# Second MLP put into the list scheduler, with a shorter product in its clock; the values of the square go to SBUF

## The chip, the cores and the metric

The kernel runs on one core of a Trainium2 chip. The metric is device time in microseconds (us), lower is better; a kernel is timed in several runs and the median counts. One further execution is recorded by the hardware profiler; its rows are the ones read here. Engines are named as the profile names them: PE is TensorE's matmul, PEld its weight load, DVE is VectorE, ACT is ScalarE, POOL is GpSimd, SP the engine that issues the DMAs.

## The reference, cut to what matters

Attention through 32 packed positions per head, then two MLPs over 4608 tokens. The change is in the second MLP, `_moe2_ref`: a product, SoLU (the input times its softmax), a layer norm, a product.

```python
def _moe_ref(x, w_in, w_out):                 # first MLP, d_ff 2048, ELU
    h = x @ w_in
    g = np.where(h > 0.0, h, np.exp(np.minimum(h, 0.0)) - 1.0)
    return g @ w_out

def _moe2_ref(x, w_in, w_out, g_ln):          # second MLP, d_ff 1024
    h = x @ w_in
    h_max = np.max(h, axis=-1, keepdims=True)
    e = np.exp(h - h_max)
    sm = e / (np.sum(e, axis=-1, keepdims=True) + 1e-09)
    solu = h * sm
    mu = np.mean(solu, axis=-1, keepdims=True)
    var = np.mean((solu - mu) ** 2, axis=-1, keepdims=True)
    ln = (solu - mu) / np.sqrt(var + 1e-06) * g_ln
    return ln @ w_out
```

## The kernel before

**Tiles.** Every fp32 product is made of three fp32r products: each operand is split into a rounded part (hi) and the rest (lo), and hi*hi, lo*hi and hi*lo are added up in PSUM. The first MLP works on half a batch of 288 tokens at a time (b, half) and on 16 blocks f of 128 hidden columns; its name for a step is b_half_f, so `fe7_1_10` is the ELU buffer of batch 7, half 1, block 10. A step is the product `h` (6 matmuls), ELU on ACT and DVE (`fe`), a split into `ghi` and `glo`, and 12 matmuls into `acc`. The result goes to DRAM in `x2_dram` and is read back as `x2raw` in tiles of 512 tokens.

**The second MLP** works on 36 tiles i of 128 tokens (NTT = 36), four to an `x2raw` tile. For each of them:

- `split_x2` (L504): hi on ACT, lo on DVE (`x2hi`, `x2lo`).
- `h2_mm` (L509): 24 matmuls of 512 columns into a PSUM tile of two banks. There are three such tiles: `misc` has one buffer and `acc` two, and the tiles take them in turn, so product i+3 takes the tile of product i (product 1 takes that of product 0).
- `solu_ln` (L520): negated row maximum (`nm`, DVE), exponential with row sum (`e`, ACT), reciprocal (`sm`, `r`, DVE), `z` = h times softmax with row sum (DVE), the square with its sum (ACT, L535), the variance (`sq`, DVE), its power -1/2 (POOL), `ln` (DVE). Of the square only its sum is used; its values were written over the product in PSUM.
- `t2_blocks` (L543): a transposition of 32x32 blocks (`lnB`, DVE) and 16 copies that put the blocks in place (`lnX`), half on DVE (L555) and half on ACT (L557).
- `t2_a` (L560): the split of the transposed tile, `lnT`: hi on ACT, lo on DVE. There are two buffers, so tile i+2 waits until product i is done.
- `out_mm` (L566): 24 matmuls `o`, the first 16 of which read only hi; a copy `y` to SBUF (ACT) and the store (SP). The last tile does its 512 columns in two halves.

**What sets the order.** The attention and the first MLP are nodes of a list scheduler (`order`, L924): each node has an engine, a duration in the planner's own clock, needs, buffers that it takes and lets go, and perhaps a due time; the scheduler lays each engine's nodes in one order that is then emitted as it stands, for PE, DVE, ACT and SP. Before the change the scheduler's last nodes were the load of the first `x2raw` tile, the splits of tiles 0 and 1, and `h2_mm(0)`. Everything behind that was called by hand at the end of the kernel (L1023 to L1048): there PE follows the written order (`h2_mm(i + 3)`, then `out_mm(i)`), while DVE, ACT, POOL and SP are ordered by the framework's own scheduler, which may also put their instructions among those of the first MLP.

Of the kernel before, what the change touches and what calls it, by code (L numbers as in the profile page):

```python
# [34 lines left out]
def attention_mlp_kernel(ctx: ExitStack, tc: tile.TileContext, q, k, v, v_tail, p,  # L35
# [484 lines left out]
    def solu_ln(i):  # L520
        o = last.pop(("h2", i)).rearrange("p a c -> p (a c)")
        nm = small.tile([P, 1], F32, tag="nm", name=f"nm2_{i}")
        dve.tensor_reduce(out=nm, in_=o, axis=AX.X, op=ALU.max, negate=True)  # L523
        e = work.tile([P, 5 * 4 * D], F32, tag="k", name=f"e3_{i}", bufs=1)[:, 0:DFF2]
        sm = small.tile([P, 1], F32, tag="sm", name=f"sm2_{i}")
        act.activation(e, o, AF.Exp, bias=nm, accum_out=sm)
        dve.tensor_scalar(out=sm, in0=sm, scalar1=1e-9, scalar2=None, op0=ALU.add)
        r = small.tile([P, 1], F32, tag="r", name=f"r2_{i}")
        dve.reciprocal(r, sm)
        z = work.tile([P, 5 * 4 * D], F32, tag="q", name=f"z{i}", bufs=1)[:, 0:DFF2]  # L530
        su = small.tile([P, 1], F32, tag="su", name=f"su{i}")
        dve.scalar_tensor_tensor(out=z, in0=o, scalar=r, in1=e, op0=ALU.mult, op1=ALU.mult, accum_out=su)  # L532
        dve.tensor_scalar(out=su, in0=su, scalar1=-1.0 / DFF2, scalar2=None, op0=ALU.mult)
        sq = small.tile([P, 1], F32, tag="sq", name=f"sq{i}")
        act.activation(o, z, AF.Square, bias=su, accum_out=sq)  # L535
        dve.tensor_scalar(out=sq, in0=sq, scalar1=1.0 / DFF2, scalar2=1e-6, op0=ALU.mult, op1=ALU.add)
        rs = small.tile([P, 1], F32, tag="rs", name=f"rs{i}")
        nc.gpsimd.tensor_tensor(out=rs, in0=sq, in1=mhalf, op=ALU.pow)
        ln = work.tile([P, DFF2], F32, tag="stage", name=f"ln{i}", bufs=2)
        dve.tensor_scalar(out=ln, in0=z, scalar1=su, scalar2=rs, op0=ALU.add, op1=ALU.mult)  # L540
        last["ln", i] = ln

    def t2_blocks(i):  # L543
# [5 lines left out]
        tv = t.rearrange("p (c a n) -> p c a n", a=4, n=NP)
        ov = o.rearrange("p (c n) -> p c n", n=P)  # L550
        for r in range(4):
            for a in range(4):
                x, y = ov[a * NP:(a + 1) * NP, :, r * NP:(r + 1) * NP], tv[r * NP:(r + 1) * NP, :, a]
                if (r + a) % 4 < 2:
                    dve.tensor_copy(x, y)  # L555
                else:
                    act.copy(x, y)  # L557
        last["t2", i] = o

    def t2_a(i):  # L560
        o = last.pop(("t2", i))
        t = slot(f"lnT{i}", [P, 2, 8, P], f"wo{6 + i % 2}", F32R)
        both(split(t[:, 0].rearrange("p c n -> p (c n)"), t[:, 1].rearrange("p c n -> p (c n)"), o))
        last["lnT", i] = t

    def out_mm(i):  # L566
        t = last.pop(("lnT", i))
        n = DM if i < NTT - 1 else DM // 2
        for c in range(0, DM, n):
            o = h_ps(f"o{i}_{c}")[:, 0:n]  # L570
            for x in range(2):
                for kk in range(8):
                    w, cs = wo2[kk // 2], slice((kk % 2) * DM + c, (kk % 2) * DM + c + n)
                    pe.matmul(o, t[:, x, kk], w[:, 0, cs], start=x + kk == 0, stop=x == 1 and kk == 7)  # L574
                    if x == 0:
                        pe.matmul(o, t[:, 0, kk], w[:, 1, cs], start=False, stop=False)  # L576
            y = work.tile([P, DM], F32, tag="at", name=f"y{i}_{c}", bufs=3)[:, 0:n]
            act.copy(y, o)
            sp.dma_start(out=out[i * P:(i + 1) * P, c:c + n], in_=y)
# [309 lines left out]
    def order():  # L889
# [194 lines left out]
```

## Time and profile before

| | before |
|---|---|
| median of 3 runs | 1145.37 us (1145.16 to 1147.82) |
| profiled execution, its own time | 1142.79 us |
| its span, first to last instruction | 1141.0 us |
| PE busy | 1114.4 us (98%) |
| DVE busy | 868.5 us (76%) |
| ACT busy | 750.7 us (66%) |
| POOL busy | 20.4 us (2%) |
| mean granted TensorE clock | 0.994 |

The profiled execution is 1.8 us longer than its span, and 2.6 us under the median of the runs. PE's busy share counts overlapping matmuls whose ends are modelled; where PE loses time is read from the starts of its matmuls. The second MLP's first product starts at 731.54 us and its last matmul at 1137.55 us.

### The profile page before, as it was taken

What the parts mean: (1) busy time and instruction counts of PE and PEld (TensorE: products, weight loads), DVE (VectorE), ACT (ScalarE), POOL (GpSimd) and SP (SyncE); (2) the same over time, 40 slices, a digit from 0 to 9 for tenths busy, and PEclk for the clock granted to TensorE, in tenths of its full rate; (3) what the DMA queues carried; (4) which work ended last, traced back from release to release, by engine and by line L of the source; (5) the groups of instructions that cost most, each with busy time, mean ns of one, the idle gap of its engine ahead of it and who ended that gap; (6) DMA issues with size and microseconds to landing.
All of it is one profiled execution on the core that took longest, in us unless ns stands there. A gap on an engine that the chain in (4) does not pass through costs nothing.

```text
span 1141.0 us, 21041 instructions
## 1 busy us (share of the span) xinstructions
PE 1114.4 (98%) x8164; PEld 984.1 (86%) x8164; DVE 868.5 (76%) x1956; ACT 750.7 (66%) x1627; POOL 20.4 (2%) x42
## 2 busy tenths in 40 slices
PE   8799999999999999999999999999999999999997
PEld 7588898899899899899899899878888888888886
DVE  5899897678777778777778644588877878878775
ACT  4688865666666765666665555567776776676674
POOL 0000000000000000000000000000000000000000
PEclk9899999999999999999999999999999999999999
DMA  9957334024133124233122322610202101000001
GB/s 344 342 174 260 105 104 125 24 82 139 59 121 121 59 103 139 77 103 121 59 101 99 111 95 65 215 52 34 65 19 65 56 28 65 19 28 20 28 28 38
DMA packets 56116, 111.07 MB, mean 97 GB/s; under 512 B 4432, under 2 KB 32336, under 8 KB 54224
## 3 DMA queue, kind: packets, MB, share of 16 engines
q1 hardware_dynamic: 56016, 109.73, 28.3%
q8 instruction: 64, 1.05, 0.4%
q14 instruction: 36, 0.29, 0.1%
HBM read 77.14 MB, written 32.57 MB: 96 GB/s over the span
## 4 chain that ended last, share of the span: by engine, by line
PE 54%; DVE 22%; ACT 15%; issue 6%; POOL 1%; DMA 1%; POOLq 0%; SPq 0%; ACTq 0%; DVEq 0%
PE acc L64 11%; PE acc L66 10%; PE acc L65 10%; ACT lnX L557 6%; PE h L64 6%; PE h L66 6%; PE h L65 6%; DVE lnB L547 4%; PE m L348 3%; DVE ln L540 2%; DVE z L532 2%; ACT h L535 2%; DVE lnT L154 2%; DVE nm L523 2%; PE s L348 2%
## 5 line engine op out<-in xcount | busy, mean ns | idle before, releaser
L64 PE MATMUL acc<-ghi,wo 128*128 128x288 f32 x1024 | 305.9, 299 | 0.6 <-DVE part L484 0.3
L66 PE MATMUL acc<-glo,wo 128*128 128x288 f32 x1024 | 301.6, 295 | 1.2 <-DVE glo L449 1.2
L65 PE MATMUL acc<-ghi,wo 128*128 128x288 f32 x1024 | 301.5, 294 | 0.0
L64 PEld LDWEIGHTS acc<-ghi,wo 128*128 128x128 f32 x1024 | 192.2, 188 | 22.0 <-ACT fe L433 9.1
L66 PEld LDWEIGHTS acc<-glo,wo 128*128 128x128 f32 x1024 | 192.4, 188 | 1.7 <-DVE glo L449 1.7
L65 PEld LDWEIGHTS acc<-ghi,wo 128*128 128x128 f32 x1024 | 192.3, 188 | 0.0
L574 PE MATMUL o<-wo,lnT 128*128 128x512 f32 (+1 forms) x592 | 185.0, 385 | 4.5 <-ACT lnT L152 4.5
L446 ACT CAST ghi<-fe 128x288 fp32r<-128x288 f32 x256 | 110.2, 431 | 103.5 <-DVE fe L439 102.7
L439 DVE SCALAR_TENSOR_TENSOR fe<-fe,h 128x288 f32<-128x288 f32 x256 | 115.3, 451 | 77.1 <-ACT fe L434 73.8
L557 ACT COPY lnX<-lnB 32x256 f32<-32x256 f32 x288 | 116.3, 404 | 78.1 <-DVE lnB L547 65.5
L64 PE MATMUL h<-AT,M 128*128 128x288 f32 x512 | 155.7, 304 | 10.6 <-DVE fe L439 9.0
L433 ACT ACTIVATE fe<-h 128x288 f32<-128x288 f32 x256 | 104.7, 409 | 91.3 <-PE h L66 85.9
L65 PE MATMUL h<-AT,M 128*128 128x288 f32 x512 | 151.6, 296 | 0.0
L66 PE MATMUL h<-AT,M 128*128 128x288 f32 x512 | 151.2, 295 | 0.3 <-DVE AT L154 0.3
L449 DVE TENSOR_TENSOR glo<-fe,ghi 128x288 fp32r<-128x288 f32 x256 | 115.3, 451 | 44.1 <-ACT ghi L446 41.8
L574 PEld LDWEIGHTS o<-wo,lnT 128*128 128x128 f32 x592 | 110.7, 189 | 27.4 <-ACT lnT L152 5.3
L64 PEld LDWEIGHTS h<-AT,M 128*128 128x128 f32 x512 | 96.3, 188 | 33.0 <-DVE fe L439 14.5
L434 ACT ACTIVATE fe<-fe 128x288 f32<-128x288 f32 x256 | 113.9, 445 | 8.0
L576 PE MATMUL o<-wo,lnT 128*128 128x512 f32 (+1 forms) x296 | 113.8, 386 | 0.0
L64 PE MATMUL h<-wi,x2hi 128*128 128x512 f32 x288 | 112.3, 390 | 1.3 <-ACT h L535 1.3
L66 PE MATMUL h<-wi,x2hi 128*128 128x512 f32 x288 | 112.1, 389 | 0.0
L65 PE MATMUL h<-wi,x2lo 128*128 128x512 f32 x288 | 112.1, 389 | 0.0
(101 smaller groups left out, 1613.5 us busy)
## 6 DMA issues: line engine op xcount, KB each, us to landing
k<-in_k SPq DMA_DIRECT2D x32, 288.0 KB, 3.5
q<-in_q SPq DMA_DIRECT2D x16, 576.0 KB, 4.5
x_dram<-x SPq DMA_DIRECT2D x32, 288.0 KB, 2.8
x2raw<-x_dram SPq DMA_DIRECT2D x9, 1024.0 KB, 5.6
out_x<-y SPq DMA_DIRECT2D x35, 256.0 KB, 2.0
raw_wi<-in_w_in SPq DMA_DIRECT2D x8, 1024.0 KB, 9.6
v<-in_v SPq DMA_DIRECT2D x16, 512.0 KB, 5.2
w_dram<-w SPq DMA_DIRECT2D x16, 512.0 KB, 2.9
```

What stands on the lines that cost most here:

```text
L64: pe.matmul(o, a[0], b[0], start=start, stop=False)
L65: pe.matmul(o, a[1], b[0], start=False, stop=False)
L66: pe.matmul(o, a[0], b[1], start=False, stop=stop)
L348: pe.matmul(o[u * NP:(u + 1) * NP, r], w[rows, u, :], x[rows, u, :], start=True, stop=True)
L433: act.activation(e, o[:, 0:HS], AF.Relu, scale=-1.0)
L434: act.activation(e, e, AF.Exp, scale=-1.0)
L439: dve.scalar_tensor_tensor(out=e, in0=e, scalar=-1.0, in1=o[:, 0:HS], op0=ALU.add, op1=ALU.max)
L446: act.copy(ghi, e)
L449: dve.tensor_tensor(out=glo, in0=e, in1=ghi.bitcast(F32), op=ALU.subtract)
L557: act.copy(x, y)
L574: pe.matmul(o, t[:, x, kk], w[:, 0, cs], start=x + kk == 0, stop=x == 1 and kk == 7)
L576: pe.matmul(o, t[:, 0, kk], w[:, 1, cs], start=False, stop=False)
```

## The change

All of the second MLP becomes nodes of the list scheduler, for all 36 tiles. `solu_ln`, `t2_blocks` and `t2_a` are cut into one function per step, POOL becomes an engine of the planner, and a product counts 4.6 us in the planner's clock (H2_US; the one node of it that was there counted 5.6). The square (L546 after) writes its values into the SBUF tile `ln`, which `so_ln` overwrites later, so the PSUM tile of the product is let go by `z` and not by the square. In the last tile 12 of the 16 block copies are DVE's, 4 ACT's. The calls by hand at the end are gone. The number of matmuls, of bytes and of the other steps stays.

```diff
+    def so_z(i):
+        z = last["z", i] = work.tile([P, 5 * 4 * D], F32, tag="q", name=f"z{i}", bufs=1)[:, 0:DFF2]
...
+    def so_sqr(i):
+        sq = last["sq", i] = small.tile([P, 1], F32, tag="sq", name=f"sq{i}")
+        ln = last["ln", i] = work.tile([P, DFF2], F32, tag="stage", name=f"ln{i}", bufs=2)
+        act.activation(ln, last["z", i], AF.Square, bias=last["su", i], accum_out=sq)
-        act.activation(o, z, AF.Square, bias=su, accum_out=sq)
...
+    ENGINES = PE, DVE, ACT, SP, POOL = "PE", "DVE", "ACT", "SP", "POOL"
+    LATENCY = {PE: 0.2, DVE: -0.02, ACT: -0.03, SP: 1.9, POOL: 0.1}
...
-    node(("h2", 0), PE, 5.6, [("spD", "x2", 0)] + [("wi2", j) for j in range(4)],
-         lambda: h2_mm(0), takes=[("misc", "h2")], due=end_due + 2)
+    end_due = FIRST_US + STEP_US * len(steps) + 2
+    H2_US = 4.6
...
+    for i in range(NTT):
+        out_due = end_due + (4 + 2 * i) * H2_US
+        h2_due = end_due + i * H2_US if i < 4 else out_due - 7 * H2_US
+        bank = ("misc" if i % 3 == 0 or i == 1 else "acc", ("h2", i))
...
+        node(("h2", i), PE, H2_US, [("spD", "x2", i)] + ([("wi2", j) for j in range(4)] if i == 0 else []),
+             lambda i=i: h2_mm(i), takes=[bank], due=h2_due,
...
+        node(("so_max", i), DVE, 1.22, [("h2", i)], lambda i=i: so_max(i))
+        node(("so_exp", i), ACT, 1.33, [("so_max", i)], lambda i=i: so_exp(i), takes=[e3])
+        node(("so_z", i), DVE, 1.5, [("so_rec", i)], lambda i=i: so_z(i), takes=[z], lets=[e3, bank])
+        node(("so_sqr", i), ACT, 1.33, [("so_z", i)], lambda i=i: so_sqr(i), takes=[ln])
...
+                eng = DVE if (r + a) % 4 < 2 or i == NTT - 1 and (r + a) % 4 < 3 else ACT
+                moves.append(node(("t2m", i, r, a), eng, 0.29 if eng == DVE else 0.4,
...
+            node(("out", i, c), PE, H2_US * n / DM, [("spD", "lnT", i)] + ([("wo2", j) for j in range(4)] if i == 0 else []),
+                 lambda i=i, c=c, n=n: out_mm(i, c, n), takes=[o], lets=[lnt], due=out_due + (c > 0) * 2.7)
...
-    ctx.enter_context(tc.manual_schedule(engines={mybir.EngineType.PE}))
-    solu_ln(0)
-    both(split_x2(2))
-    h2_mm(1)
...
-        out_mm(i)
```

What the scheduler makes of it is seen in the order of instructions. On PE the order is the same up to the end of the first MLP; there `h` of step 7_1_15 now stands ahead of the second MLP's first product and no longer behind it; products 5 to 8 each stand one place earlier among the `o` products (h2_3, o_0, h2_4, h2_5, o_1, h2_6, o_2, h2_7, o_3, h2_8, o_4, o_5, h2_9, o_6), and from there on the order is that of before. On SP `x2raw1`, the second tile of 512 tokens, was issued ahead of the two halves of `wo2_3`, the last weights of the second product, and now stands behind them.

The first place is ACT's queue in the last steps of the first MLP (`x2hi0` and `x2hi1` are hi of the first and second 512 tokens, `e3_0` the exponential of the second MLP's tile 0). Before:

```order
L433 ACTIVATE fe7_1_10_9541<-h7_1_10_9521 128x288
L152 CAST x2hi0_9472<-x2raw0_9470 128x4x128 x2
L434 ACTIVATE fe7_1_10_9541<-fe7_1_10_9541 128x288
L152 CAST x2hi0_9472<-x2raw0_9470 128x4x128
L446 CAST ghi7_1_10_9546<-fe7_1_10_9541 128x288
L152 CAST x2hi0_9472<-x2raw0_9470 128x4x128
L433 ACTIVATE fe7_1_11_9574<-h7_1_11_9549 128x288
L152 CAST x2hi1_9840<-x2raw1_9838 128x4x128 x4
L434 ACTIVATE fe7_1_11_9574<-fe7_1_11_9574 128x288
```

After, to the same step's ELU and then at the end of the first MLP:

```order
L433 ACTIVATE fe7_1_10_9541<-h7_1_10_9521 128x288
L434 ACTIVATE fe7_1_10_9541<-fe7_1_10_9541 128x288
L152 CAST x2hi0_9472<-x2raw0_9470 128x4x128
L446 CAST ghi7_1_10_9546<-fe7_1_10_9541 128x288
L152 CAST x2hi0_9472<-x2raw0_9470 128x4x128
...
L433 ACTIVATE fe7_1_15_9704<-h7_1_15_9671 128x288
L434 ACTIVATE fe7_1_15_9704<-fe7_1_15_9704 128x288
L446 CAST ghi7_1_15_9708<-fe7_1_15_9704 128x288
L152 CAST x2hi1_9649<-x2raw1_9647 128x4x128 x4
L528 ACTIVATE e3_0_9734,sm2_0_9735<-h2_0_9679,nm2_0_9732 128x1024
```

The splits of `x2raw0` moved behind both halves of the ELU of step 7_1_10 and stand one at a time between the steps; the four of `x2raw1` moved from the middle of step 7_1_11 to behind the last step.

The second place is the end of DVE's queue, the second MLP's tiles 34 and 35 (`lnB` is the transposition, `nm2` the maximum, `lnX` the block copies, `lnT` the lo part that the product needs). Before:

```order
L547 STREAM_TRANSPOSE lnB34_13033<-ln34_12973 128x1024
L523 TENSOR_REDUCE nm2_35_13052<-h2_35_13005 128x1
L555 COPY lnX34_13035<-lnB34_13033 32x8x32 x8
L527 TENSOR_SCALAR sm2_35_13055<-sm2_35_13055 128x1
L529 RECIPROCAL r2_35_13058<-sm2_35_13055 128x1
L532 SCALAR_TENSOR_TENSOR z35_13060,su35_13061<-h2_35_13005,r2_35_13058,e3_35_13054 128x1024
L533 TENSOR_SCALAR su35_13061<-su35_13061 128x1
L154 TENSOR_TENSOR lnT34_13099<-lnX34_13035,lnT34_13099 128x1024
```

After:

```order
L565 STREAM_TRANSPOSE lnB34_13029<-ln34_13013 128x1024
L523 TENSOR_REDUCE nm2_35_13056<-h2_35_12985 128x1
L576 COPY lnX34_13058<-lnB34_13029 32x8x32 x2
L154 TENSOR_TENSOR lnT33_13026<-lnX33_12964,lnT33_13026 128x1024
L533 TENSOR_SCALAR sm2_35_13061<-sm2_35_13061 128x1
L534 RECIPROCAL r2_35_13067<-sm2_35_13061 128x1
L576 COPY lnX34_13058<-lnB34_13029 32x8x32
L539 SCALAR_TENSOR_TENSOR z35_13072,su35_13073<-h2_35_12985,r2_35_13067,e3_35_13060 128x1024
L541 TENSOR_SCALAR su35_13073<-su35_13073 128x1
L576 COPY lnX34_13058<-lnB34_13029 32x8x32 x5
```

The copies of tile 34 are spread around the steps of tile 35, and the lo part of tile 33 stands where DVE had waited for the exponential. The same pattern fills nearly all tiles from 10 on. The third place is ACT's queue beside it, the same two tiles. Before:

```order
L557 COPY lnX34_13035<-lnB34_13033 32x8x32 x8
L526 ACTIVATE e3_35_13054,sm2_35_13055<-h2_35_13005,nm2_35_13052 128x1024
L578 COPY y32_0_13096<-o32_0_13071 128x512
L152 CAST lnT34_13099<-lnX34_13035 128x1024
L535 ACTIVATE h2_35_13005,sq35_13064<-z35_13060,su35_13061 128x1024
```

After:

```order
L528 ACTIVATE e3_35_13060,sm2_35_13061<-h2_35_12985,nm2_35_13056 128x1024
L574 COPY lnX34_13058<-lnB34_13029 32x8x32 x7
L546 ACTIVATE ln35_13107,sq35_13106<-z35_13072,su35_13073 128x1024
L594 COPY y32_0_13113<-o32_0_13031 128x512
L574 COPY lnX34_13058<-lnB34_13029 32x8x32
L152 CAST lnT34_13120<-lnX34_13058 128x1024
```

The exponential of tile 35 moved from behind the eight copies of tile 34 to ahead of them.

## Rows read from the trace of the kernel before

**Rows 1.** Stretches: PE, PEld, DVE, ACT, POOL busy (x instructions), clock, DMA, GB/s.
```profile
780.00:1108.00 328.00, 328.00 (x1448) 271.69 (x1448) 265.81 (x565) 226.40 (x446) 16.45 (x30) 1.00 0.11 37
1119.00:1132.00 13.00, 8.53 (x30) 6.23 (x29) 8.48 (x22) 9.69 (x20) 0.55 (x1) 0.87 0.12 42
```
**Rows 2.** Timeline of PE, first MLP's end: start, us, instruction [idle before <-releaser].
```profile
717.45 0.30 PE L64 MATMUL h<-AT,M 128*128 128x288 f32 x1
...
719.83 0.29 PE L64 MATMUL h<-AT,M 128*128 128x288 f32 x1
...
722.46 0.40 PE L64 MATMUL h<-AT,M 128*128 128x288 f32 x1
...
726.65 0.40 PE L64 MATMUL h<-AT,M 128*128 128x288 f32 x1 [1.55 <-DVE fe L439]
```
**Rows 3.** Timeline of PE, from the first MLP's last matmul to o_0.
```profile
742.46 0.29 PE L66 MATMUL acc<-glo,wo 128*128 128x288 f32 x1
743.52 0.50 PE L64 MATMUL h<-wi,x2hi 128*128 128x512 f32 x1 [0.77 <-ACT h L535]
...
755.22 0.50 PE L64 MATMUL h<-wi,x2hi 128*128 128x512 f32 x1 [0.51 <-ACT h L535]
...
760.79 0.39 PE L574 MATMUL o<-wo,lnT 128*128 128x512 f32 x1
```
**Rows 4.** Timeline of PE: h2_35, o_32, o_34 and o_35 start.
```profile
1103.51 0.39 PE L64 MATMUL h<-wi,x2hi 128*128 128x512 f32 x1
...
1108.95 0.39 PE L574 MATMUL o<-wo,lnT 128*128 128x512 f32 x1
...
1122.59 0.50 PE L574 MATMUL o<-wo,lnT 128*128 128x512 f32 x1 [2.60 <-ACT lnT L152]
...
1131.83 0.39 PE L574 MATMUL o<-wo,lnT 128*128 128x256 f32 x1 [1.88 <-ACT lnT L152]
```
**Rows 5.** Timeline of ACT, splits of `x2raw0` and `x2raw1`.
```profile
720.09 1.14 ACT L152 CAST x2hi<-x2raw 128x512 fp32r<-128x512 f32 x2 [1.24 <-DMA x2raw<-x_dram]
...
723.60 2.17 ACT L152 CAST x2hi<-x2raw 128x512 fp32r<-128x512 f32 x4
```
**Rows 6.** Timeline of DVE, end of the queue: tile 34's and tile 35's maximum.
```profile
1105.64 1.19 DVE L523 TENSOR_REDUCE nm<-h 128x1 f32<-128x1024 f32 x1
...
1114.44 0.81 DVE L540 TENSOR_SCALAR ln<-z,su,rs 128x1024 f32<-128x1024 f32 x1 [0.73 <-POOL rs L538]
...
1116.46 1.19 DVE L523 TENSOR_REDUCE nm<-h 128x1 f32<-128x1024 f32 x1
```
**Rows 7.** Timeline of ACT, tile 35: copies of tile 34, exponential, hi of tile 35.
```profile
1116.57 3.31 ACT L557 COPY lnX<-lnB 32x256 f32<-32x256 f32 x8 [3.04 <-DVE lnB L547]
1119.91 1.11 ACT L526 ACTIVATE e<-h,nm 128x1024 f32<-128x1024 f32 x1
...
1130.73 1.04 ACT L152 CAST lnT<-lnX 128x1024 fp32r<-128x1024 f32 x1
```
**Rows 8.** Timeline of DVE, tile 0's maximum and `z`.
```profile
737.22 1.23 DVE L523 TENSOR_REDUCE nm<-h 128x1 f32<-128x1024 f32 x1 [2.29 <-PE h L66]
...
740.72 1.28 DVE L532 SCALAR_TENSOR_TENSOR z<-h,r,e 128x1024 f32<-128x1024 f32 x1
```
**Rows 9.** Timeline of SP's queue: `x2raw0` and `x2raw1`, `wo2_3`.
```profile
712.19 5.98 SPq L499 DMA_DIRECT2D x2raw<-x_dram  x2
720.82 0.88 SPq L197 DMA_DIRECT2D wo<-w_dram  x2
```
**Rows 10.** Groups from 700 us on: busy us, mean ns | idle before, releasers.
```profile
L555 DVE COPY lnX<-lnB 32x256 f32<-32x256 f32 x288 | 81.5, 283 | 3.6
...
L547 DVE STREAM_TRANSPOSE lnB<-ln 128x1024 f32<-128x1024 f32 x36 | 44.8, 1245 | 1.1
L154 DVE TENSOR_TENSOR lnT<-lnX,lnT 128x1024 fp32r<-128x1024 f32 x36 | 44.1, 1224 | 10.7 <-ACT lnT L152 10.7
...
L535 ACT ACTIVATE h<-z,su 128x1024 f32<-128x1024 f32 x36 | 40.2, 1117 | 30.3 <-DVE su L533 30.3
```

More of the change, by code (lines that the diff above doesn't have):

```diff
@@ L527, in solu_ln, with so_rec @@
+    def so_rec(i):
+        sm = last.pop(("sm", i))
+        r = last["r", i] = small.tile([P, 1], F32, tag="r", name=f"r2_{i}")
         dve.tensor_scalar(out=sm, in0=sm, scalar1=1e-9, scalar2=None, op0=ALU.add)
-        r = small.tile([P, 1], F32, tag="r", name=f"r2_{i}")
         dve.reciprocal(r, sm)
-        z = work.tile([P, 5 * 4 * D], F32, tag="q", name=f"z{i}", bufs=1)[:, 0:DFF2]
-        su = small.tile([P, 1], F32, tag="su", name=f"su{i}")
-        dve.scalar_tensor_tensor(out=z, in0=o, scalar=r, in1=e, op0=ALU.mult, op1=ALU.mult, accum_out=su)
@@ L549, in t2_blocks @@
[L549 to L579, printed above, removed]
@@ L585, in attention_mlp_kernel, with t2_move @@
-    ENGINES = PE, DVE, ACT, SP = "PE", "DVE", "ACT", "SP"
+    def t2_move(i, r, a, eng):
+        if ("lnX", i) not in last:
+            last["lnX", i] = big.tile([P, 4 * HS], F32, tag="AT", name=f"lnX{i}", bufs=3)[:, 0:DFF2]
+        tv = last["lnB", i].rearrange("p (c a n) -> p c a n", a=4, n=NP)
+        ov = last["lnX", i].rearrange("p (c n) -> p c n", n=P)
+        x, y = ov[a * NP:(a + 1) * NP, :, r * NP:(r + 1) * NP], tv[r * NP:(r + 1) * NP, :, a]
+        if eng is act:
+            act.copy(x, y)
+        else:
+            dve.tensor_copy(x, y)
@@ new lines, in t2_split, with out_mm @@
+    def t2_split(i):
+        t = last["lnT", i] = slot(f"lnT{i}", [P, 2, 8, P], f"wo{6 + i % 2}", F32R)
+        return split(t[:, 0].rearrange("p c n -> p (c n)"), t[:, 1].rearrange("p c n -> p (c n)"), last.pop(("lnX", i)))
+    def out_mm(i, c, n):
+        t = last["lnT", i]
+        o = last["y", i, c] = h_ps(f"o{i}_{c}")[:, 0:n]
+        for x in range(2):
+            for kk in range(8):
+                w, cs = wo2[kk // 2], slice((kk % 2) * DM + c, (kk % 2) * DM + c + n)
+                pe.matmul(o, t[:, x, kk], w[:, 0, cs], start=x + kk == 0, stop=x == 1 and kk == 7)
+                if x == 0:
+                    pe.matmul(o, t[:, 0, kk], w[:, 1, cs], start=False, stop=False)
@@ L586, in attention_mlp_kernel, with y_copy, y_store @@
+    def y_copy(i, c, n):
+        y = work.tile([P, DM], F32, tag="at", name=f"y{i}_{c}", bufs=3)[:, 0:n]
+        act.copy(y, last.pop(("y", i, c)))
+        last["y", i, c] = y
+    def y_store(i, c, n):
+        sp.dma_start(out=out[i * P:(i + 1) * P, c:c + n], in_=last.pop(("y", i, c)))
+    ENGINES = PE, DVE, ACT, SP, POOL = "PE", "DVE", "ACT", "SP", "POOL"
     CAPS = dict(misc=1, acc=2, h=2, fe=2, ghi=4, glo=4, at=3, AT=3, cv=2, stage=2, xo=2)
-    LATENCY = {PE: 0.2, DVE: -0.02, ACT: -0.03, SP: 1.9}
+    LATENCY = {PE: 0.2, DVE: -0.02, ACT: -0.03, SP: 1.9, POOL: 0.1}
```

94 lines of the change are left out of this document (51 added, 43 removed).

## The prediction

> **What bounds the kernel now.** I read the busy time of each engine by stretches first, then the starts of PE's matmuls where a stretch is not full, then, around each hole, the queue of the engine that PE waited for. In the stretch from 780 to 1108 us PE is busy in 328.00 of 328.00 us, at a granted clock of 1.00 [rows 1]. A product of 24 matmuls takes 5.44 us there, from the start of h2_35 at 1103.51 to that of o_32 at 1108.95 [rows 4], so a tile, with its two products, takes PE 10.88 us. The matmuls stay what they are, so nothing can be gained in this stretch. What can be gained are holes, and they lie in three places.
>
> First, the last steps of the first MLP. The product h of two steps starts 2.38 us apart when nothing waits (717.45 to 719.83); the next two follow at 722.46 and 726.65, that is 2.63 and 4.19 us later [rows 2]. Lost: 0.25 + 1.81 = 2.06 us. The wait is for DVE's `fe`, and the reason stands in ACT's queue: at 720.09 two `x2hi` casts that waited 1.24 us for the load of `x2raw0`, and at 723.60 four more of 2.17 us for the second tile of tokens [rows 5], each between the two halves of one step's ELU, as the order shows.
>
> Second, the first products of the second MLP. h2_1 starts at 743.52, 1.06 us after the last matmul before it instead of the 0.13 us at which such matmuls follow each other (18 of them in a step's 2.38); from h2_1 to h2_3 it is 11.70 us instead of 2 x 5.44 = 10.88; from h2_3 to o_0 5.57 instead of 5.44 [rows 3]. Lost: 0.93 + 0.82 + 0.13 = 1.88 us. Both waits are for ACT L535, the square, which still wrote over the product in the one `misc` tile.
>
> Third, the end. o_32 starts at 1108.95; o_35, three products later, would start at 1108.95 + 16.32 = 1125.27 and starts at 1131.83 [rows 4]. Lost: 6.56 us. o_34 and o_35 both wait for hi of `lnT`, 2.60 and 1.88 us. In the stretch 1119 to 1132 the granted clock is 0.87 [rows 1]: with levels of 2.4 and 1.2 GHz that is 26% of 13 us at the lower one, 3.4 us, of which half, 1.7 us, is loss. PE had stood still for 2.60 us before the clock fell, so this is part of the same hole. The cause is a lag. h2_35 is done at 1108.95, yet its maximum starts at 1116.46 [rows 6], 7.5 us later, with no wait in front of it: DVE came to it late. DVE's round, from tile 34's maximum to tile 35's, takes 1116.46 - 1105.64 = 10.82 us [rows 6], just under PE's 10.88, so a lag once there is never worked off. While PE has products of other tiles it costs nothing; after the last h2 it is the path.
>
> **The change, part by part.**
>
> *Splits of x2.* The `x2raw0` casts move behind the first ELU half; the wait for the load now hides in slack, since the ELU of 7_1_10 is done before it and `glo` of that step is wanted only at the end of the product h of 7_1_12, about 723.0. The cast that starts at 720.09 delays `ghi` by 0.6 us to about 721.1. The four casts for the second tile go behind step 7_1_15. What is late next: `x2raw1` is now behind `wo2_3` in SP's queue. That load starts at 720.82 and takes SP 0.88 us [rows 9], so `x2raw1` is issued at about 721.7 and no longer at 717.6 (the end of the merged row, 718.17, less one issue). The nearest row for its flight is `x2raw0`, also issued right behind 1 MB of weights: 712.19 to 720.09, 7.9 us, hence 729.6. By my walk PE then runs from 719.83 without a hole: four h-and-acc pairs of 2.38 (the steps 11 to 14 of half 1) and h of 7_1_15 (0.8) bring h2_0 to about 730.2, and ACT reaches the four casts at about 732.2, two microseconds of ELU later. Margin 2.6 us. I take the loss of 2.06 as gone; the ends are nothing gained, and all of it.
>
> *Bank of h2.* h2_0 runs 730.2 to 735.6; twelve matmuls each for three steps end at 740.4. In the trace h2_0 ended at 731.54 + 5.44 = 736.98, the maximum started 0.24 us later, and `z` ended 4.78 us after that start (740.72 + 1.28 - 737.22) [rows 8], with an ELU step in between on both engines that is now gone. So `z` lets the bank go at 740.6 at worst, some 0.5 us sooner without that ELU, and PE wants it at 740.4; the square, on the path before, is off it. For h2_3 the same 5.0 us after h2_1's end at 745.8 make 750.8, and it is wanted at 751.3. I take 1.88 as gone. The ends: zero, and 1.88. Sum of both at the start: 3.94, o_0 at about 756.9 and not 760.79.
>
> The square's own time: on the row SBUF to PSUM takes 1117 ns [rows 10]; the cast of the same 128x1024, SBUF to SBUF, takes 1040 [rows 7]. I cost the new destination at nothing; at 0.1 us it would be hidden under ACT's slack (226.40 of 328 us busy [rows 1]) in all but the last tile. The Trainium skill (ScalarE: Activation LUTs, Step-by-step: what each stage is for) says that ScalarE writes faster to PSUM than to SBUF, a rule against this edit; by it the square would grow, and the sum would lose that once, at the end. The two rows do not show such a difference.
>
> *Order in the steady stretch.* DVE is busy 265.81 us in 328, 8.8 us a tile [rows 1]. Its round of 10.82 holds 2.0 us of waits: some 1.2 for the exponential, which stood behind eight copies on ACT, 0.73 for POOL and the rest for the square. In the new order the lo part of an older tile, 1224 ns [rows 10], fills the first wait, and the exponential stands ahead of the copies. My round: 8.8 + 0.73 + 0.2 = 9.7 us. Bounds: 8.8 with no wait, 10.82 with all. Either is under 10.88, and DVE now starts without a lag, since the maxima of tiles 1 to 3 wait for PE. So each maximum starts when its product ends, and PE never waits: hi of tile i is ready before h2_(i+2) ends, a product and more ahead of o_i.
>
> *End.* Let E be the end of h2_35, and count from E. DVE: maximum 0.2 to 1.3 (the next instruction starts 1.11 behind it), two copies at 0.29 to 1.9, lo of 33 to 3.1, two small steps and a copy to 3.8, `z` to 5.2, row sum 5.3, five copies 6.8. ACT: exponential 1.5 to 2.7, seven copies at 0.41 to 5.6, square to 6.8, `y32` 7.4, one copy 7.8, hi of 34 to 8.9. o_34 wants that at 10.88: no wait. DVE goes on: variance 7.2, POOL, `ln` 7.9 to 8.75, transposition 1245 ns [rows 10] to 10.0, three copies 10.9, lo of 34 12.2 (its product wants lo after 16 matmuls, at 14.5), nine copies 14.9; ACT hi of 35, 1.04 [rows 7], to 16.0. o_35 wants it at 16.32: no wait, by 0.3 us. The 12 copies on DVE cost 3.5 us and not 2.35, but ACT's four end at 13.4 and were the longer side. So all 6.56 us go, the lower clock too, as PE no longer stands still. Ends: zero if a lag of 7 us stays, 6.56 if none does.
>
> *Sum.* 2.06 + 1.88 + 6.56 = 10.5 us. Against the profiled execution, 1142.79 - 10.5 = 1132.3. The runs' median lies 2.6 us above that execution, so I carry the difference over to it: 1145.37 - 10.5 = **1134.9 us**, 0.9% less.
>
> **Rivals.** *A, the start gives nothing.* `x2raw1` lands late, and DVE and ACT stand in queue: both have its four splits ahead of tile 0's maximum and exponential, so every microsecond of landing after 732.2 is PE's. For it: the load moved 4 us back, behind 1 MB. Against it: the 2.6 us of margin. At 4 us of delay the 3.94 are gone: 1145.4 - 6.6 = 1138.8.
>
> *B, the end gives nothing.* A lag of DVE arises again in tiles 4 to 8, where the new order has the maximum of tile 6 ahead of that of tile 5 and mixes in the splits of the third token tile, and stays. Against it: a round of 9.7 works off 1.2 us a tile. 1145.4 - 3.9 = 1141.4.
>
> *C, slower.* The new round of DVE and ACT is longer than PE's 10.88, since each engine stands in its one queue for steps of three tiles at once. Then each of 34 tiles adds the excess to the lag, and the end pays it all: at 11.5 us it is 34 x 0.62 = 21 us in place of the 6.6 of now, 1145.4 - 3.9 - 6.6 + 21 = 1156. It loses from a round of 10.88 + 10.5/34 = 11.2 on. Against it: the sum of the steps is 1.5 us short of that.
>
> *D, no change.* In tiles 4 to 8 PE meets products whose `lnT` is not ready, o_4 and o_5, which now follow each other with no h2 between: my walk has hi of tile 5 some 5 us ahead of its product, and the planner's 4.6 us against the true 5.44 makes it think DVE scarcer than it is, not less so. If both wait a whole product, 10.9 us, the gain is eaten: 1145.8.
>
> **How the numbers follow.** Forecast 0.70, with a range of its own of 1132 to 1138; A 0.12, B 0.07, C 0.05, D 0.06. The range 1131.5 to 1140.5 holds forecast and A, and leaves out B, C and D, 0.18. About 0.3%, 3.4 us, is what a measurement here can tell from no change: faster means under 1141.9. Forecast, A and most of B (0.05) are faster: 0.87. The rest of B and D are the same: 0.08. C is slower: 0.05.
>
> **What would show it.** In the new profile h of 7_1_11 to 7_1_15 start 2.38 us apart; no PE wait names the square; o_0 starts at 757 or so; the maximum of a late tile starts within 0.5 us of its product's end, with a wait for PE in front of it; o_34 and o_35 have no wait in front, and the clock is 1.00 to the end. It would be wrong if the four casts of `x2raw1` wait for a DMA, if DVE's round is over 10.88, or if a PE wait for `lnT` shows up among o_1 to o_6.

## The result and the profile after

The changed kernel takes 1134.13 us (median of 5 runs, 1132.46 to 1135.35), the kernel before, run beside it, 1145.37 us (5 runs, 1144.6 to 1147.82): ratio 0.9898, 95% interval 0.9882 to 0.9914, 11.2 us less. The forecast was 1134.9.

The profiled execution of after is 1135.35 us long with a span of 1133.6 us, only 7.4 us less than before's 1141.0. The rest of the difference lies ahead of everything that the change touches. The product h of step 7_1_10, which in both kernels follows the same PE instructions, starts at 717.45 us in before's trace [rows 2] and at 720.67 in after's. From there to the end of the span before takes 423.55 us and after 412.93: 10.62 us less, where 10.5 were forecast. The 3.2 us are taken up under the last heading. Below, stretches of two traces are compared from a common instruction, not by the clock of the span.

The two stretches of [rows 1] in after's trace, and between them a third, from 1111 to 1124 us, up to the last tile:

```profile
780.00:1108.00 328.00, 328.00 (x1449) 271.70 (x1448) 276.35 (x577) 233.23 (x452) 20.74 (x31) 1.00 0.13 45
1111.00:1124.00 13.00, 13.00 (x59) 10.78 (x58) 10.59 (x28) 8.99 (x18) 0.55 (x1) 1.00 0.11 40
1119.00:1132.00 13.00, 11.41 (x73) 10.24 (x72) 5.05 (x12) 4.58 (x9) 0.00 (x0) 1.00 0.17 59
```

PE is full to 1124 and beyond, at a clock of 1.00; the last line includes the end, where there is nothing left to do. The steps of the first MLP, which answer to [rows 2], are evenly spaced at 2.38 to 2.40 us:

```profile
720.67 0.30 PE L64 MATMUL h<-AT,M 128*128 128x288 f32 x1
...
723.05 0.30 PE L64 MATMUL h<-AT,M 128*128 128x288 f32 x1
...
725.45 0.30 PE L64 MATMUL h<-AT,M 128*128 128x288 f32 x1
...
727.83 0.30 PE L64 MATMUL h<-AT,M 128*128 128x288 f32 x1
```

h2_1 and o_0, which answer to [rows 3], and o_32 and its predecessor h2_35, to [rows 4]. None has a wait in front of it:

```profile
743.55 0.30 PE L66 MATMUL acc<-glo,wo 128*128 128x288 f32 x1
743.68 0.39 PE L64 MATMUL h<-wi,x2hi 128*128 128x512 f32 x1
...
760.02 0.39 PE L588 MATMUL o<-wo,lnT 128*128 128x512 f32 x1
...
1102.74 0.39 PE L64 MATMUL h<-wi,x2hi 128*128 128x512 f32 x1
...
1108.18 0.39 PE L588 MATMUL o<-wo,lnT 128*128 128x512 f32 x1
```

ACT's splits of `x2raw0` and `x2raw1` (compare [rows 5]): the first still waits for its load, but behind the ELU; the four of the second follow the last step and wait for nothing.

```profile
722.11 0.45 ACT L434 ACTIVATE fe<-fe 128x288 f32<-128x288 f32 x1
723.22 0.62 ACT L152 CAST x2hi<-x2raw 128x512 fp32r<-128x512 f32 x1 [0.66 <-DMA x2raw<-x_dram]
...
735.36 2.18 ACT L152 CAST x2hi<-x2raw 128x512 fp32r<-128x512 f32 x4
```

DVE at the end (compare [rows 6]). The maximum of tile 35 now stands waiting for PE; before it started 7.5 us late with no wait:

```profile
1097.50 1.22 DVE L523 TENSOR_REDUCE nm<-h 128x1 f32<-128x1024 f32 x1 [1.21 <-PE h L66]
...
1108.38 1.23 DVE L523 TENSOR_REDUCE nm<-h 128x1 f32<-128x1024 f32 x1 [1.22 <-PE h L66]
...
1120.32 2.68 DVE L576 COPY lnX<-lnB 32x256 f32<-32x256 f32 x9
```

And ACT's hi of tile 35 (compare [rows 7]), which o_35 waits for:

```profile
1123.08 1.05 ACT L152 CAST lnT<-lnX 128x1024 fp32r<-128x1024 f32 x1 [1.56 <-DVE lnX L576]
```

It ends at 1124.13 and o_35 starts at 1108.18 + 16.32 = 1124.50, on time, with 0.37 us to spare.

What DVE waited for between 900 and 1100 us shows where the lag comes from (waits by line; total us, times, longest). Before:

```profile
DVE sm L527 <- ACT e L526: 13.5, 11, 1.2
DVE ln L540 <- POOL rs L538: 10.5, 14, 1.1
DVE sq L536 <- ACT h L535: 7.7, 14, 1.4
...
```

After:

```profile
DVE nm L523 <- PE h L66: 15.3, 16, 2.4
DVE ln L558 <- POOL rs L554: 9.8, 17, 0.7
DVE sq L550 <- ACT ln L546: 0.8, 1, 0.8
```

Before, DVE waited 21 us for ACT's exponential and square, and never for PE. After, these waits are down to 0.8 us, and the time that they gave back shows as a wait for PE: in the late tiles DVE is early in each round. (A round is the time from one tile's maximum to the next tile's.)

### The profile page after: what moved, and what is told of

Same layout as the page of the kernel before. It is cut to its first block, busy times and chain, and to the rows that moved or that the text cites. A ratio compares the mean times of both kernels' runs of the same rounds, so it can differ in the third digit from the quotient of the medians.

```text
span 1133.6 us, 20979 instructions
## 1 busy us (share of the span) xinstructions
PE 1113.6 (98%) x8164; PEld 985.9 (87%) x8164; DVE 874.2 (77%) x1960; ACT 751.4 (66%) x1623; POOL 24.2 (2%) x42
## 4 chain that ended last, share of the span: by engine, by line
PE 88%; DVE 6%; ACT 3%; issue 1%; DMA 1%; SPq 1%; DVEq 0%; ACTq 0%
PE o L588 12%; PE h L64 12%; PE acc L64 11%; PE h L65 11%; PE h L66 11%; PE acc L66 11%; PE acc L65 11%; PE o L590 6%; PE m L348 3%; PE s L348 2%; DMA q<-in_q 1%; PE pp L328 1%; DVE fe L439 1%; DVE glo L449 1%; ACT fe L434 1%
```

## The experiments

Medians are of runs; what a part costs is read from the trace as the time from one PE instruction to another, which repeats to a few hundredths of a microsecond. The three stretches are: h2_0 to o_0, o_0 to o_32, and o_32 to the end of the span. The lag is the time from a product's end to its maximum's start; 0.2 us is none. "More" and "less" are against the second measurement of the changed kernel (after, again), unless another kernel is named. The kernels were measured on three chips, where the kernel before had medians of 1145.37 to 1146.13 us, so less than a microsecond between two medians decides nothing.

| kernel | median us | h2_0 to o_0 | o_0 to o_32 | o_32 to end | lag of tile 35's maximum |
|---|---|---|---|---|---|
| before | 1145.37 | 29.25 | 348.16 | 32.04 | 7.5 |
| after, again | 1133.75 | 26.61 | 348.16 | 25.39 | 0.2 |
| sq_psum | 1138.58 | 31.93 | 348.16 | 25.39 | 0.2 |
| x2_early | 1137.06 | 26.58 | 348.16 | 25.38 | 0.2 |
| clock_544 | 1141.56 | 26.61 | 348.16 | 33.50 | 9.5 |
| sq_only | 1143.13 | 27.85 | 348.16 | 33.02 | 7.1 |
| exp_late | 1152.28 | 26.61 | 353.96 | 39.23 | 12.2 |
| lumped | 1133.42 | 26.61 | 348.16 | 25.39 | 0.2 |
| both_old | 1156.53 | 26.61 | 356.87 | 38.82 | 12.2 |
| clock_500 | 1134.31 | 26.61 | 348.16 | 25.43 | 0.2 |
| clock_420 | 1136.38 | 32.05 | 342.72 | 27.48 | 1.1 |
| pad_1 | 1135.31 | 26.61 | 348.16 | 25.91 | 0.2 |
| last_8 | 1134.27 (one run) | 26.61 | 348.16 | 25.39 | 0.2 |

**The base.** The changed kernel again, as it is.

> The changed kernel once more, as the base of the others on one chip. Both theories: 1134.1 us (range of its five runs 1132.5 to 1135.4). In the trace, from h of step 7_1_10 to the span's end 412.9 us, within 0.3. If the stretch ahead of it (720.7 us in the first profile, 717.5 in the kernel before, with the same instructions there) comes out between these two, its 3.2 us are spread of the start-up and no cost of the change; if it stays at 720.7 the change costs something there that the order doesn't show.

1133.75 us (1133.14 to 1134.05); from h of step 7_1_10 on 412.9 us. That step starts at 719.19, between the two, so the start-up is spread and not a cost of the change. (sq_only below, which has the order of before there, starts it at 720.76.)

**The bank, undone** (sq_psum):

```diff
-        act.activation(ln, last["z", i], AF.Square, bias=last["su", i], accum_out=sq)
+        act.activation(last.pop(("o", i)), last["z", i], AF.Square, bias=last["su", i], accum_out=sq)
```

> The changed kernel with the square's values written over the product in PSUM again, so that the bank is let go by the square and not by z; the order of instructions stays. Theory (the bank is what the first products wait for): z ends 0.4 us before PE wants the bank for h2_1, the square ends about 1.4 us later, so h2_1 starts about 1.0 us late; h2_3 likewise, at most 2 us; together 1.5 to 3.3 us more, about 1136.5, all of it before o_0. Rival 1 (the destination's own price decides, the steady stretch does the rest): the square is 0.03 us shorter, no loss, 1134. Rival 2 (the bank is needed late in all rounds): several us more, with PE waits for the square in the steady stretch too.

1138.58 us, 4.8 more, all of it ahead of o_0 (5.32 in the trace). The place was right; the size was not. The timeline of PE, h2_1 and h2_3, the stretch from then on, and ACT's queue ahead of the square of tile 1:

```profile
742.12 0.53 PE L64 MATMUL h<-wi,x2hi 128*128 128x512 f32 x1 [0.95 <-ACT h L546]
...
755.52 0.65 PE L64 MATMUL h<-wi,x2hi 128*128 128x512 f32 x1 [2.17 <-ACT h L546]
```

```profile
755.00:764.00 9.00, 8.48 (x30) 6.91 (x31) 4.56 (x9) 2.81 (x6) 0.55 (x1) 0.81 0.00 1
```

```profile
753.28 1.04 ACT L152 CAST lnT<-lnX 128x1024 fp32r<-128x1024 f32 x1 [1.13 <-DVE lnX L576]
754.23 1.11 ACT L546 ACTIVATE h<-z,su 128x1024 f32<-128x1024 f32 x1
```

h2_1 starts 1.11 us late, h2_2 0.17 later still and h2_3 another 2.33. Then the clock falls: 0.81 on average over those 9 us, with levels of 2.4 and 1.2 GHz, and product h2_3 takes 7.15 us in place of 5.44. The expectation had counted the holes, at 3.3 us at most where they are 3.61, and not the 1.71 us that follow the second one. The second hole is the larger because hi of `lnT` of tile 0 now stands ahead of the square of tile 1 in ACT's queue: the square starts 6.28 us after that tile's maximum (754.23 - 747.95), where it was 4.61 in the kernel before (753.92 - 749.31). The changed kernel has the same order, but there PE does not wait for the square.

**The bank alone** (sq_only, made from the kernel before):

```diff
-        act.activation(o, z, AF.Square, bias=su, accum_out=sq)
+        ln = work.tile([P, DFF2], F32, tag="stage", name=f"ln{i}", bufs=2)
+        act.activation(ln, z, AF.Square, bias=su, accum_out=sq)
```

> The kernel before with one part of the change alone: the square writes its values into ln in SBUF, so that z lets the bank of the product go; all else, the calls by hand too, as before. Theory: the holes at h2_1 and h2_3 (0.93 and 0.82 us) go, and no more than that, since the splits among the last ELU steps (2.06 us) and the lag at the end (6.56 us) stay: about 1143.6, 1.7 us less. Rival 1: most of the gain comes from the bank, since DVE may run ahead in every round: 1138 or less. Rival 2: the bank is late by DVE's own queue, so nothing: 1145.4.

1143.13 us, ratio to before 0.9983 (0.9970 to 0.9996), that is 0.5 to 3.4 us less, which holds the 1.7 us expected. In the trace h2_0 to o_0 shrinks by 1.40, and no PE wait names the square any more; one of 0.2 us for `z` is left. The end stays bad, as expected; it is even 0.98 longer (33.02) than in before's trace, so that from h of step 7_1_10 on this execution, one of the slowest of the ten (1145.75), won only 0.4 us. The size of this part is therefore known only roughly.

**The splits, undone** (x2_early):

```diff
+        early = [("x2raw", 1)] + [("spA", "x2", i) for i in range(4, 8)] + [("spD", "x2", i) for i in range(4, 8)]
+        plan = [x for x in plan if x not in early]
+        pos = next(n for n, x in enumerate(plan) if x == ("wo2", 3))
+        plan.insert(pos, early[0])
+        pos = next(n for n, x in enumerate(plan) if x == ("fx", 7, 1, 11))
+        plan[pos:pos] = early[1:5]
+        pos = next(n for n, x in enumerate(plan) if x == ("gl", 7, 1, 12))
+        plan[pos + 1:pos + 1] = early[5:]
```

> The changed kernel with one part undone: the load of the second 512 tokens stands ahead of the last weights of the second product again, and its four splits stand in front of the ELU of step 7_1_11 on ScalarE and behind step 7_1_12's split on VectorE, as in the kernel before; all else as changed. Theory (the four casts, 2.17 us in ScalarE's queue, delay the ELU): h of a step between 7_1_12 and 7_1_14 starts 1.5 to 2.1 us late, everything behind it as much later, about 1136. Rival (the loss was made by the casts that waited 1.24 us for the first 512 tokens, which stay where the change put them): 1134, with steps 2.38 us apart.

1137.06 us (1135.97 to 1139.89), 3.3 more; in the trace 4.5, all between h of 7_1_12 and h2_0. ACT's queue there, then PE at h of 7_1_13, 7_1_14 and 7_1_15, and the stretch:

```profile
726.38 2.18 ACT L152 CAST x2hi<-x2raw 128x512 fp32r<-128x512 f32 x4 [1.82 <-DMA x2raw<-x_dram]
728.46 0.40 ACT L433 ACTIVATE fe<-h 128x288 f32<-128x288 f32 x1
```

```profile
729.88 0.40 PE L64 MATMUL h<-AT,M 128*128 128x288 f32 x1 [1.88 <-DVE fe L439]
...
733.90 0.30 PE L64 MATMUL h<-AT,M 128*128 128x288 f32 x1
...
737.02 0.40 PE L64 MATMUL h<-AT,M 128*128 128x288 f32 x1 [0.57 <-DVE fe L439]
```

```profile
725.00:738.00 13.00, 10.55 (x66) 10.09 (x65) 6.74 (x13) 7.30 (x17) 0.00 (x0) 0.87 0.28 98
```

The theory's mechanism is there and the rival (no loss) is not. The steps from 7_1_12 on start 4.42, 4.02 and 3.12 us apart in place of 2.38 to 2.40. The first is the hole that was expected, 2.04 us. It is not made quite as before: there one half of the ELU stood ahead of the four casts, here neither does, so the casts' wait for the load (1.82 us) counts too. In the second step PE does not wait at all. Most of its matmuls start 0.24 us apart and not 0.13, since the clock has fallen to its lower level (0.87 on average over the 13 us), and that costs 1.62 us more, which the expectation did not count. The hole in the kernel before, 1.55 us in front of 7_1_13, had left the clock at 1.00 (726 to 740 us). The third, 0.74, is DVE's, where the four `x2lo` wait 1.06 us for PE to free a buffer and stand ahead of `fe`.

**The planner's clock.** Three kernels, with one number changed (5.44, 5.0, 4.2):

```diff
-    H2_US = 4.6
+    H2_US = 5.44
```

> The changed kernel with a product of the second MLP counted at 5.44 us in the planner's clock, its true length, and not 4.6. Theory (the gain comes from the list order as such and the due times, not from the short product): no PE wait for lnT or the square in the steady stretch, each late maximum starts within 0.5 us of its product's end, 1134 within 1 us. Rival (the short product is what pulls the work of VectorE and ScalarE ahead, with the true one steps are put off until they are due): the maxima lag by several us at the end as in the kernel before, up to 6.6 us more, 1136 to 1141.

1141.56 us, 7.8 more: the theory fell, the rival was right. All of it is in the end (33.50 against 25.39), where o_34 waits 4.97 us for hi of `lnT` and the clock is then 0.79 (1122 to 1130 us), and the maxima lag by 5.0 us at tile 10 and 9.5 at tile 35, so a round takes some 11.06 us. What DVE waits for, from 900 to 1100 us, and the place in one round:

```profile
DVE ln L558 <- POOL rs L554: 13.9, 19, 1.1
DVE sq L550 <- ACT ln L546: 12.8, 10, 1.4
DVE sm L533 <- ACT e L528: 0.9, 5, 0.2
```

```profile
1075.95 0.15 DVE L541 TENSOR_SCALAR su<-su 128x1 f32<-128x1 f32 x1
1077.47 0.15 DVE L550 TENSOR_SCALAR sq<-sq 128x1 f32<-128x1 f32 x1 [1.37 <-ACT ln L546]
```

It is the square, not the exponential. In the order that the true length makes, DVE's eight copies are all done by the time `z` is: four fill the wait for the exponential, and none is left to fill that for the square. In the changed kernel's order five copies stand between `su` and `sq`, the lo part of an older tile fills the other wait, and the square costs 0.8 us in all.

> The changed kernel with a product counted at 5.0 us in the planner's clock, between 4.6 and the 5.44 that cost 8 us. In the order that this makes, five of a tile's eight copies stand ahead of the next exponential on ScalarE, not eight; VectorE fills the wait with the lo part of the tile before. Theory (what decides is whether the order leaves VectorE a wait that lifts its round over 10.88 us): five copies end 2.05 us after the transposition, while the maximum ends at about 2.1, so the exponential isn't late, the round is 9.7 us, lag under 0.5 us at the last tiles, 1134 within 1.5 us. Rival (the planner must believe VectorE the bound: its own sum of VectorE's work is 9.4 us a tile, so any count of a product over 4.7 lets the lag grow): 1137 to 1141.

1134.31 us, no lag: the rival (any count over 4.7 loses) fell. Its waits show a round under PE's in the same way, with four copies between `su` and `sq`:

```profile
DVE ln L558 <- POOL rs L554: 10.9, 18, 0.7
DVE nm L523 <- PE h L66: 10.2, 11, 0.9
DVE sq L550 <- ACT ln L546: 1.1, 7, 0.2
```

> The changed kernel with a product counted at 4.2 us in the planner's clock. Theory (a shorter count only packs VectorE and ScalarE tighter; PE has no wait to lose): no lag at the end, 1134 within 1.5 us unless the first products come out in another place. Rival (with the products due too early the order puts products of lnT ahead of the time when lnT is there): PE waits for lnT among the first ten tiles, 2 us and more, 1136 or more.

1136.38 us, 2.6 more (2.1 in the trace), and neither expectation holds. There is no PE wait among the first ten tiles (h2_4 stands ahead of o_0 there, which moves 5.44 us from one column of the table to the next and costs nothing); there is one at the end:

```profile
1120.17 0.50 PE L588 MATMUL o<-wo,lnT 128*128 128x512 f32 x1 [1.78 <-ACT lnT L152]
```

The last tiles come a little late here (a lag of 1.1 us at tile 35, with rounds of 9.7 to 12.5 us). That a tighter clock sets the steps of more tiles between each other is a likely reason, but it was not traced.

**The exponential behind the copies** (exp_late):

```diff
+        for i in range(10, NTT):
+            n = plan.index(("so_exp", i))
+            late = [x for x in plan[n:] if not isinstance(x, int) and x[0:2] == ("t2m", i - 1) and (x[2] + x[3]) % 4 >= 2]
+            if ("t2", i - 1) in plan[:n]:
+                plan = plan[:n] + late + [x for x in plan[n:] if x not in late]
```

> The changed kernel with the exponential of a tile put behind all copies of the tile before in ScalarE's queue, from tile 10 on, wherever it stood ahead of them, as in the kernel before; VectorE's order stays. Theory (the place of the exponential is what keeps VectorE's round under PE's): the eight copies take 3.3 us from the transposition's end, the exponential then ends 4.45 us after the maximum's start, and VectorE wants it at 3.0: 1.45 us of wait in a round of 9.66, so 11.1 us in those rounds, over PE's 10.88. The maxima then lag more with each such tile, 3 to 5 us at the last, and the end is as much longer: 1137 to 1139. Rival (the lag came from the rounds in which four splits of x2 stood together, and the exponential's place is covered by the slack of 1.2 us): 1134 to 1135, lag under 1 us.

1152.28 us, 18.5 more, slower than before (ratio 1.0059, 1.0042 to 1.0076). The mechanism is the expected one, but the loss is some four times the 3 to 5 us expected. In one round:

```profile
995.68 3.32 ACT L574 COPY lnX<-lnB 32x256 f32<-32x256 f32 x8
999.02 1.12 ACT L528 ACTIVATE e<-h,nm 128x1024 f32<-128x1024 f32 x1
```

```profile
996.97 1.22 DVE L154 TENSOR_TENSOR lnT<-lnX,lnT 128x1024 fp32r<-128x1024 f32 x1
1000.26 0.15 DVE L533 TENSOR_SCALAR sm<-sm 128x1 f32<-128x1 f32 x1 [2.06 <-ACT e L528]
```

The wait is 2.06 us, not 1.45, the plain late rounds take 11.3 us, and those that hold splits mostly 11.9 to 12.8. Waits for the exponential come to 32.1 us between 900 and 1100. From a lag of some 11 us on, PE waits for `lnT` in the steady stretch too (353.96 and not 348.16). The expectation had taken rounds of 11.1 for a part of the tiles. The kernel before had this same order on ACT and a round of 10.82: there DVE did its own eight copies in that wait. What counts is that the two queues fit.

**The splits in lumps** (lumped), and **both** (both_old: the two edits together):

```diff
+        for t in range(3, NTT * P // BLK):
+            for kind in ("spA", "spD"):
+                four = [(kind, "x2", i) for i in range(4 * t, 4 * t + 4)]
+                n = min(plan.index(x) for x in four)
+                plan = [x for x in plan[:n] if x not in four] + four + [x for x in plan[n:] if x not in four]
```

> The changed kernel with the four splits of each tile of 512 tokens standing together on ScalarE and on VectorE, as in the kernel before, from the fourth such tile on; all else as changed. Theory: one round in four grows from about 9.7 by three splits of 0.6 us to about 11.4 us, and the next one works off the 0.5 us over 10.88 with its 1.2 us of slack: no change, 1134 to 1135. Rival (the lumps alone build the lag): lag of several us at the last tiles, 1137 to 1140.

1133.42 us, no change, to the hundredth in the trace. A lump (the four splits together) makes a maximum late by up to 1.4 us, here 12.24 us behind the one before, and the next one comes after 9.55 us and has caught up:

```profile
1031.47 1.23 DVE L523 TENSOR_REDUCE nm<-h 128x1 f32<-128x1024 f32 x1 [1.22 <-PE h L66]
...
1038.07 2.50 DVE L154 TENSOR_TENSOR x2lo<-x2raw,x2hi 128x512 fp32r<-128x512 f32 x4
...
1043.71 1.19 DVE L523 TENSOR_REDUCE nm<-h 128x1 f32<-128x1024 f32 x1
...
1053.26 1.19 DVE L523 TENSOR_REDUCE nm<-h 128x1 f32<-128x1024 f32 x1
```

> The changed kernel with both of the former orders in the second MLP: the exponential behind the copies of the tile before, and the four splits of 512 tokens together. Theory (rounds over 10.88 in most tiles, and one in four of over 12 us): the lag grows to 6 us and more at the end, all of the loss at the end of the kernel before or more of it: 1139 to 1143. Rival (the lag has another cause, such as the framework's order of VectorE): under 1137.

1156.53 us: 22.8 more than after, where exp_late alone is 18.5 and lumped nothing. The expectation had 5 to 9 us more, so it had the sign and not the size. Without slack the lumps cost 4.3 (2.5 in the trace, from o_0 to the end).

**One more DVE instruction per tile** (pad_1):

```diff
+        for _ in range(1):
+            dve.tensor_scalar(out=ln, in0=ln, scalar1=1.0, scalar2=0.0, op0=ALU.mult, op1=ALU.add)
```

> The changed kernel with one more instruction of VectorE in each tile, a multiplication of ln by one and addition of zero, 0.82 us, in front of the transposition. Theory (VectorE waits 1.2 us for PE in each late round): the round without that wait grows from 9.66 to 10.5, still under 10.88, so the steady stretch stays at 348.16 us from o_0 to o_32 and the maxima still start within 1 us of their products' ends; at the end 0.5 to 1.5 us more, since the chain of the last two tiles is longer by two such instructions and has a margin of 0.4: 1135. Rival (the slack is not there, each round is bound by VectorE's chain): 36 times 0.8 us of lag, 1150 and more.

1135.31 us; in the trace 0.52 more, all in the end, as expected. The instruction takes 0.69 us, and the wait for PE shrinks from 1.22 to 0.48:

```profile
1105.93 0.69 DVE L561 TENSOR_SCALAR ln<-ln 128x1024 f32<-128x1024 f32 x1
...
1108.39 1.22 DVE L523 TENSOR_REDUCE nm<-h 128x1 f32<-128x1024 f32 x1 [0.48 <-PE h L66]
```

**The last tile's copies** (last_8):

```diff
-                eng = DVE if (r + a) % 4 < 2 or i == NTT - 1 and (r + a) % 4 < 3 else ACT
+                eng = DVE if (r + a) % 4 < 2 else ACT
```

> The changed kernel with the last tile's sixteen copies shared eight and eight between VectorE and ScalarE, as in the kernel before, and not twelve and four. Theory: VectorE's copies of tile 35 end 1.2 us sooner and ScalarE's end at 1119.87 + 8 x 0.41 = 1123.2 in the changed kernel's time, against 1123.08 where hi of tile 35 starts there; so o_35 starts as before, within 0.2 us, and from o_32 to the end it is 25.4 us. Rival (ScalarE is the longer side): 1 us more there.

25.39 us from o_32 to the end, the same. Hi of tile 35 is ready 0.2 us ahead of o_35 and not 0.4. That edit bought no time.

## Why the prediction was right, and where its reasons were not

**The sum.** The forecast was 10.5 us, and from h of step 7_1_10 on the traces show 10.62, in the three places that it named. That the median came within 0.8 us of the forecast is partly luck: the five runs lie between 1132.46 and 1135.35, and the profiled execution, forecast at 1132.3, took 1135.35, since its start-up was 3.2 us longer.

**The steady stretch.** o_0 to o_32 is 348.16 us in both kernels: PE-bound, as forecast. DVE's round was forecast at 9.7; in late tiles it is 10.88 - 1.22 = 9.66, and pad_1 shows that the slack is real, since 0.74 us more a tile are swallowed. What the prediction had wrong here is that each maximum starts when its product ends. In the early tiles many do not, though PE never waits for them: tile 8's maximum starts 5.6 us after its product, tile 5's 12.2, as the order sets it behind that of tile 6 and DVE waits 2.47 us for PE first. From tile 20 on none is left. So a lag as in rival B did arise, and the slack worked it off, which is what the prediction had set against B.

**Splits of x2.** Forecast 2.06, and the even steps show all of it gone. The load `x2raw1` went out at 724.97, as forecast some 4.3 us after h of 7_1_10, where it had been 0.15 in the kernel before. It was there in time (some 7.8 us later, 2.5 us ahead of its casts at 735.36): rival A did not happen. x2_early confirms that the four casts of `x2raw1` and their wait, in front of an ELU, hold up PE by some 2 us; the two casts of `x2raw0` (0.25 us) were not undone by themselves.

**Bank of h2.** Forecast 1.88; with the splits 3.94 to o_0, against 43.34 - 39.35 = 3.99 in the traces (from h of 7_1_10). The attribution was too simple: in the old order the new destination brings 1.40 us, while in the new order going without it costs 5.32. Three things had made it dearer. First, h of step 7_1_15 now stands ahead of h2_0 and no longer between h2_0 and h2_1, so PE comes to h2_1 0.78 us sooner (4.83 us after h2_0's end and not 5.61, holes left out), and the square of tile 0 is sooner by only 0.60. Second, and for more, the square of tile 1 now stands behind hi of `lnT` of tile 0; that is most of why h2_1 to h2_3 takes 13.40 us in sq_psum and took 11.70 in the kernel before. Third, the clock falls behind the longer hole, which is the 1.71 us. The prediction walked through the new order rightly (`z` at the bank just in time, 743.3 for 743.68) but priced the edit by the holes of the old one.

**The square's destination** was costed at nothing. By the profile's groups it is not quite nothing (after):

```profile
L546 ACT ACTIVATE ln<-z,su 128x1024 f32<-128x1024 f32 x36 | 41.5, 1153 | 11.1 <-DVE su L541 10.4
```

1153 ns to SBUF against 1117 to PSUM [rows 10]; the other two kernels with the one edit agree (sq_only 1152 to SBUF, sq_psum 1119 to PSUM). So the rule of the Trainium skill (ScalarE: Activation LUTs, Step-by-step: what each stage is for), that ScalarE writes PSUM faster than SBUF, holds here, by 36 ns of 1117; the prediction, which had compared the square with a cast, saw no difference. It does not show in the time: from o_32 to the end, where the sum would have lost it, sq_psum and after both take 25.39 us.

**The end.** Forecast 6.56, measured 32.04 - 25.39 = 6.65. The walk was close: o_35 was to have 0.3 us to spare and has 0.37; hi of 34 was to be ready 2.0 us ahead and is. But of the lag's origin the prediction had half. That a lag once there is never worked off is right; what makes it grow, it did not say. Before, the maxima lag 0.2 us at tile 2, 4.1 at tile 9, 6.8 at tile 25, and the rounds repeat 12.32, 10.83, 10.82, 10.22: 0.67 us over four of PE's each time. The 10.82 that the prediction took for the round is that of the last tiles, which hold no splits. The four splits of a token tile stand in the round of 10.22; the normalized rows (`ln`) and the transposition of the tile before, which would have come in it, follow in the next, that of 12.32. The two together are 0.78 us over two of PE's, the other two 0.11 under. Yet the lumps are not the cause alone: with slack in the round they cost nothing (lumped), without it they do (both_old).

**Which part of the change.** The prediction took the list order for the cause and the 4.6 us only as a risk, in rival D. The expectation of clock_544 even held the number for harmless, and that fell: with the true 5.44 the same scheduler gives an end 1.5 us worse than before's, and all that remains is the gain at the start (1141.56). So the short product is what removes the lag. The prediction's number did not suffer from this, since it had walked through the order that 4.6 makes. It is not a matter of the planner thinking DVE scarcer than PE, since 5.0 does as well (two products are then 10.0 us, over the planner's 9.4 for DVE's work on a tile); 5.44 makes an order in which nothing is left to stand in DVE's wait for the square. That 4.2 costs 2 us again says that the number is tuned by what comes out, not derived. Which of the planner's rules puts the copies there for 5.44 was not traced.

**Rivals B, C and D** did not happen: B's lag did not stay, and PE waits for `lnT` nowhere. C's mechanism was seen in exp_late, where rounds of 11.3 us and more cost 18.5 us.

## What to carry to other kernels

When one engine is full, look at whether the engine that feeds it waits for it: a wait of VectorE for TensorE of a microsecond a round is the margin that absorbs lumps, while a round within 1% of TensorE's (10.82 us against 10.88) stores each disturbance until the end, where it is paid at once. Price an edit by the slack that it has in the order that the other edits make, not in the old one: the same one-line change was worth 1.4 us in one order and 5.3 in the other, 1.7 of that by the lower clock behind the hole. And a planner's cost is a knob, not a measurement; a true one can give the worse order.

## What the runs showed of the hardware that had not been expected

**The start-up varies.** In the 14 traces h of step 7_1_10 starts between 717.45 (before) and 720.76 us (sq_only), though the instructions ahead of it are in the same order; after has 720.67 and x2_early 720.68, sq_psum 718.0. The difference arises in the first 75 us: the eleventh product h of the first MLP starts at 69.93 us in before's trace and at 73.21 in after's, and from then on the two differ by 3.2 to 3.3 us. It goes with what the DMAs moved from 30 to 60 us: 339 GB/s in before's trace, 335 in sq_psum's (that product at 70.60), 318 in the second of after (71.78), 312 in the first, 307 in sq_only's (73.24) and 303 in x2_early's (73.30). It is larger than most effects measured here; a difference of two spans alone would have put the gain at 7.4 us and not 10.6. What makes the loads slower in some executions is left open.

**A hole can cost more than itself, and its length alone does not tell.** The hole of 2.17 us in sq_psum was followed by a product 1.71 us longer, at a clock of 0.81. That of 1.88 us in x2_early was followed by 4.02 us at a clock of 0.58 (729.88 to 733.90), in which a step of 2.40 us took 1.62 us more. But 1.55 us in before (at 726.65), 1.78 in clock_420 (at 1120.17) and even 2.21 in sq_only (at 1124.2) left the clock at 1.00 over the 8 us and more that followed, as did before's two of 0.77 and 0.51 (742 to 768 us). What decides between them is not shown here.
